# First attention of a fused linear-attention and MLP kernel: two token halves from the output products on, and small products of zeros in front

## The chip, the core and the metric

The kernel runs on one NeuronCore of a Trainium2 chip. A core has a matrix engine (TensorE, "PE" in the profile; its weight loads are "PEld"), a vector engine (VectorE, "DVE"), a scalar engine (ScalarE, "ACT"), a general engine (GpSimd, "POOL") and SyncE ("SP"), which issues transfers. Each engine works through a list of instructions of its own, and they wait for each other by semaphores. Transfers between the large memory (HBM) and the on-chip memory (SBUF) run on 16 DMA engines. Products land in a third memory, PSUM[...].

The metric is the device time of one execution in microseconds (us), the median of several. The profile is of one execution; its span is slightly shorter than the timed value.

## What is computed

```python
# q, k, v: (8, 8, 576, 64)   batch, heads, sequence, head dimension
kv  = np.einsum('bhsd,bhse->bhde', k, v)
out = np.einsum('bhsd,bhde->bhse', q, kv)
rms = np.sqrt(np.mean(out * out, axis=-1, keepdims=True) + 1e-06)
x   = out / rms * g_norm          # then (B,H,S,D) -> (B*S, H*D) = (4608, 512)
h   = x @ w_in                    # (512, 2048)
y   = np.maximum(0.01 * h, h) @ w_out
```

It is attention without a softmax, each head's output is divided by its root mean square, and a two-layer MLP follows. The weights `w_in` and `w_out` arrive as float64 numbers; the kernel rounds them to float32 itself, in two steps on ScalarE and four on VectorE for each block of weights. All products are float32; each shows in the trace as two records (two passes).

## The kernel before

The 4608 tokens are worked in nine blocks of 512. Block 0 is done plainly; blocks 1 to 8 use a Strassen scheme that the change leaves alone. Before block 0's MLP can start, the first 512 rows of x must be there, and that is the work of `first_attention`, on which everything waits.

Its parts, in program order (names as in the trace; "..." marks cuts):

```python
def load_first():
    # 12 loads of 288 KB (q, k, v of four pairs of heads) on three queues:
    # ScalarE ("a"), SyncE ("s") and GpSimd ("g")
    ...

zeros = view(g_all[0], 0, NT)                 # NT = 512
nc.vector.memset(zeros[:, :64], 0.0)
nc.vector.memset(zeros[:, 64:], 0.0)
...
load_w(0, nc.sync, nc.scalar)                 # first block of w_in ("stage"), 4 transfers of 128 KB

def first_attention():
    idle = ps_m.tile([P, NT], F32, tag="hd", name="idle_ps")

    def keep_warm(n=NT):
        matmul(idle[:, :n], lhsT=zeros[:, :P], rhs=zeros[:, :n], start=True, stop=True)

    keep_warm()
    keep_warm()
    ...
    for p in range(NP):                       # NP = 4 pairs of heads
        ...                                   # TensorE transposes q ("q_ps", "rest_ps"),
        ...                                   # ScalarE and VectorE copy it into qT
    for m in range(2):
        if m:
            keep_warm()
        attention_kv(0, m, kv_ps)             # the kv products
    ...
    copy_kv(0, kv_ps)                         # VectorE, kv_ps -> kv
```

From there, the part that the change regroups. `e` is one of two halves of the head dimension (32 of 64), `l` one of two heads of a pair, `half` one of two halves of the 512 tokens (N2 = 256 each), and `pin` keeps an instruction in program order on its engine (every product is pinned too):

```python
    for e in range(2):
        o_products(0, 0, NT, e, o_ps[e])      # "o_ps": 16 products of 512 columns

    w0 = rounding(0)                          # a generator: one step of rounding at each next()
    for e in range(2):
        for l in range(2):
            pin(nc.scalar.activation(squares[e][l], o_ps[e][l], func=AF.Square))        # "sq"
            if e == 0:
                pin(nc.vector.tensor_scalar(x[:, 2 * l, :], o_ps[0][l], g_sb[:, 0:1], None,
                                            op0=ALU.mult))
    for half in range(2):
        add_up(half)                          # TensorE: sums over a head ("sum_ps<-sq,group")
    next(w0, None); next(w0, None)            # ScalarE: "add", "cut"
    for half in range(2):
        root(half)                            # ScalarE: square root ("flat")
    for l in range(2):
        pin(nc.scalar.activation(x[:, 2 * l + 1, :], o_ps[1][l], func=AF.Copy, scale=g_sb[:, 1:2]))
    for half in range(2):
        turn(half)                            # TensorE: "sum_ps<-ident,flat"
    next(w0, None); next(w0, None)            # VectorE: clamp, shift
    invert(0)                                 # VectorE: reciprocal ("roots")
    spread(0)                                 # TensorE: "inv_ps<-ident,roots", 16 products
    next(w0, None)                            # VectorE: sign
    invert(1)
    spread(1)
    for _ in w0:                              # VectorE: last step
        pass
    for half in range(2):
        for l in range(2):
            scale(half, l)                    # VectorE: x times the spread reciprocals
    for j in range(1, 5):
        round_w(j)                            # further blocks of weights
```

(The two `next` on one line stand on lines of their own in the kernel.) Then the MLP of block 0 begins, "h_ps" being the product with `w_in` and "o_acc" that with `w_out`; the first of them, n = 0, is itself made in two token halves:

```python
    for n in range(2 * NC * U + 1):
        ...
        parts = 2 if n == 0 else 1
        for part in range(parts):
            cols = slice(part * NT // parts, (part + 1) * NT // parts)
            for e in range(NE):               # NE = 4
                matmul(h_ps[:, cols], lhsT=w1_sb[h][c][:, u, e, :], rhs=x[:, e, cols], ...)
        ...                                   # ScalarE: leaky ReLU; then the product with w_out of n - 1
```

Of the kernel before, what the change touches and what calls it, by code (L numbers as in the profile page):

```python
# [9 lines left out]
F32 = mybir.dt.float32  # L10
U32 = mybir.dt.uint32
I64 = mybir.dt.int64
AF = mybir.ActivationFunctionType
AX = mybir.AxisListType
ALU = mybir.AluOpType
# [8 lines left out]
def kernel(  # L24
# [36 lines left out]
    nc = tc.nc  # L61
    B, H, S, D = q.shape
    DM, DF = w_in.shape
    P = 128
    NE = DM // P
    E = 32
# [3 lines left out]
    NT = 4 * P  # L70
    NB = B * S // NT
    N2 = NT // 2
# [15 lines left out]
    ps_m = ctx.enter_context(tc.tile_pool(name="ps_m", bufs=1, space=bass.MemoryType.PSUM))  # L88

    pin = tc.keep_in_program_order  # L90
# [14 lines left out]
    def view(t, lo, *shape):  # L105
        n = 1
        for d in shape:
            n *= d
        t = t[:, lo:lo + n]
        names = "abcd"[:len(shape)]  # L110
        return t.rearrange(f"p ({' '.join(names)}) -> p {' '.join(names)}",
                           **dict(zip(names, shape))) if len(shape) > 1 else t
# [4 lines left out]
    def matmul(*args, **kw):  # L117
        pin(nc.tensor.matmul(*args, **kw))  # L118
# [4 lines left out]
    def half_of(p, i):  # L123


        return i ^ (p & 1)
# [58 lines left out]
    zeros = view(g_all[0], 0, NT)  # L185
# [26 lines left out]
    def load(t, src, eng):  # L212

        if len(src.shape) == len(t.shape):
            t, src = [t], [src]
        else:
            n = src.shape[1]
            t = [t[i * n:(i + 1) * n] for i in range(src.shape[0])]
        for i, (to, part) in enumerate(zip(t, src)):
            pin(eng[i * len(eng) // len(t)].dma_start(to, part))  # L220

    def load_f64(src, eng):
        a, n = src.shape[-2:]
        n //= 2
        raw = next(raw_homes).bitcast(U32).rearrange("p (n two) -> p n two", two=2)
        load(raw.rearrange("p (a n) two -> p a (n two)", a=a), src, eng)
        return raw
# [42 lines left out]
    def load_w(j, *eng):  # L270
        eng = eng or (nc.sync,)
        dst, src = w_jobs[j]
        if w_in.dtype == I64:
            w_raws[j] = load_f64(src.bitcast(U32), eng)
        else:
            load(dst, src, eng)
# [5 lines left out]
    def round_w(j):  # L282
        for _ in rounding(j):
# [8 lines left out]
    nc.vector.memset(group, 0.0)  # L292
    nc.vector.tensor_reduce(group[:, :NP], ident.rearrange("p (a i) -> p a i", i=E), axis=AX.X,
                            op=ALU.add)
    load_w(0, nc.sync, nc.scalar)
    g_sb = consts.tile([P, 2], F32, name="g_sb")
    for p in range(NP):
        pin(nc.gpsimd.dma_start(g_sb[p * E:(p + 1) * E], g_norm.rearrange("(e i) -> i e", i=E)))
# [35 lines left out]
    def o_products(b, lo, hi, e, o_ps):  # L334
        for p in range(NP):
            for l in range(2):
                r = slice(64 * l, 64 * l + 64)
                matmul(o_ps[half_of(p, l)][E * p:E * p + E, :],
                       lhsT=kvs[b % 2][r, p, E * e:E * e + E],
                       rhs=qTs[b][r, p, lo - b * S:hi - b * S], start=True, stop=True)  # L340
# [124 lines left out]
    def first_attention():  # L465


        idle = ps_m.tile([P, NT], F32, tag="hd", name="idle_ps")

        def keep_warm(n=NT):  # L470
            matmul(idle[:, :n], lhsT=zeros[:, :P], rhs=zeros[:, :n], start=True, stop=True)

        keep_warm()
        keep_warm()
        qT = qTs[0] = work.tile([P, NP, S], F32, tag="qT", name="qT")
        kv_ps = kv_tiles()


        rest = ps_m.tile([64, NP, P], F32, tag="oc", name="rest_ps")
        for j in range(1, 3):  # L480
            load_w(j)

        def move(p, l, to, of):

            c = 64 * half_of(p, l)
            eng = (nc.scalar.copy, nc.vector.tensor_copy)[l]
            eng(qT[c:c + 64, p, :].rearrange("p (t j) -> p j t", j=J)[:, to, :],
                of[:, :, 64 * l:64 * l + 64])

        for p in range(NP):  # L490
            q_in = q_ins.pop((0, p))
            banks = [ps_m.tile([64, 4, P], F32, tag=t, name="q_ps")
                     for t in (("ha", "hb"), ("hc", "oa"))[p % 2]]
            for j in range(J):
                to = banks[j // 4][:, j % 4, :] if j < 8 else rest[:, p, :]
                pin(nc.tensor.transpose(to, q_in[:, j, :], ident))
            for i in range(2):
                for l in range(2):
                    move(p, l, slice(4 * i, 4 * i + 4), banks[i])
        for p in range(NP):  # L500
            for l in range(2):
                move(p, l, slice(8, 9), rest[:, p:p + 1, :])
# [3 lines that stand above are left out]
            attention_kv(0, m, kv_ps)  # L506
        for j in range(3, 7):
            load_w(j)
        copy_kv(0, kv_ps)


        x = block(0)

        o_ps = [[ps_m.tile([P, NT], F32, tag=t, name="o_ps") for t in tags]
                for tags in (("hb", "hd"), ("oa", "oc"))]
        squares = [[spare(NT, "sq") for _ in range(2)] for _ in range(2)]
        roots = [work.tile([P, 2, 2, NP], F32, tag="rms", name="roots", bufs=2) for _ in range(2)]
        flat = [work.tile([64, N2], F32, tag="t2k", name="flat", bufs=3) for _ in range(2)]
        sum_ps = [ps_att.tile([P, NT], F32, tag="att", name="sum_ps") for _ in range(2)]
        inv_ps = [ps_m.tile([P, 2, N2], F32, tag=t, name="inv_ps") for t in ("ha", "hc")]  # L520
        for e in range(2):
            o_products(0, 0, NT, e, o_ps[e])

        def add_up(half):

            cols = slice(half * N2, half * N2 + N2)
            for e in range(2):
                for l in range(2):
                    matmul(sum_ps[half][E * l:E * l + E, :N2], lhsT=group,
                           rhs=squares[e][l][:, cols], start=(e == 0), stop=(e == 1))  # L530

        def root(half):

            pin(nc.scalar.activation(flat[half], sum_ps[half][:64, :N2], func=AF.Sqrt,
                                     scale=1.0 / D, bias=eps_sb[:64]))

        def turn(half):
            for t in range(2):
                matmul(turned(half)[:, t, :, :], lhsT=flat[half][:, t * P:t * P + P],
                       rhs=ident[:64, :64].rearrange("p (l i) -> p l i", l=2)[:, :, :NP],  # L540
                       start=True, stop=True)

        def turned(half):
            return sum_ps[half][:, N2:N2 + 4 * NP].rearrange("p (t l a) -> p t l a", t=2, l=2)

        def invert(half):
            pin(nc.vector.reciprocal(roots[half], turned(half)))

        def spread(half):

            for l in range(2):
                for t in range(2):
                    for p in range(NP):
                        matmul(inv_ps[half][E * p:E * p + E, l, t * P:t * P + P],
                               lhsT=roots[half][:, t, l, p:p + 1].to_broadcast([P, E]),
                               rhs=ident, start=True, stop=True)

        def scale(half, l):
            to = x[:, 2 * l:2 * l + 2, half * N2:half * N2 + N2]
            pin(nc.vector.tensor_tensor(  # L560
                to, to, inv_ps[half][:, l, :].unsqueeze(1).to_broadcast([P, 2, N2]), op=ALU.mult))

        w0 = rounding(0)
        for e in range(2):
            for l in range(2):
                pin(nc.scalar.activation(squares[e][l], o_ps[e][l], func=AF.Square))
                if e == 0:
                    pin(nc.vector.tensor_scalar(x[:, 2 * l, :], o_ps[0][l], g_sb[:, 0:1], None,
                                                op0=ALU.mult))
        for half in range(2):  # L570
            add_up(half)
        next(w0, None)
        next(w0, None)
        for half in range(2):
            root(half)
        for l in range(2):
            pin(nc.scalar.activation(x[:, 2 * l + 1, :], o_ps[1][l], func=AF.Copy,
                                     scale=g_sb[:, 1:2]))
        for half in range(2):
            turn(half)  # L580
        next(w0, None)
        next(w0, None)
        invert(0)
        spread(0)
        next(w0, None)
        invert(1)
        spread(1)
        for _ in w0:
            pass
        for half in range(2):  # L590
            for l in range(2):
                scale(half, l)
        for j in range(1, 5):
            round_w(j)

# [465 lines left out]
    x_sides, _, sums, _ = sides_x(1)  # L1061
# [34 lines left out]
    for i in range(1, NB):  # L1096
# [4 lines left out]
        for c in range(NC):  # L1101
# [76 lines left out]
            n = (i - 1) * NC + c  # L1178
# [36 lines left out]
```

## Time and profile before

| | |
|---|---|
| time, median of 3 | 919.92 us (919.35 to 920.18) |
| span of the profiled execution | 917.5 us |
| TensorE busy | 909.3 us, 99% of the span |
| VectorE busy | 631.9 us, 69% |
| GpSimd busy | 370.3 us, 40% |
| ScalarE busy | 328.4 us, 36% |
| HBM read, written | 172.39 MB, 26.48 MB |

A row of the profile's chain has a start, a duration (both us) and what ran, with the number of pieces merged into it. A row of the timeline has a start, a duration, the engine, the line of the kernel, the operation, and the tiles written and read. A row of the table by stretches has the stretch, its length, then for each engine the busy time and in brackets the number of instructions (TensorE, weight loads, VectorE, ScalarE, GpSimd), then TensorE's granted clock as a share of full speed, the busy share of the DMA engines and GB/s. L118 is the helper through which every product goes, so products are told apart by their tiles.

### The profile page before, as it was taken

What the parts mean: (1) busy time and instruction counts of PE and PEld (TensorE: products, weight loads), DVE (VectorE), ACT (ScalarE), POOL (GpSimd) and SP (SyncE); (2) the same over time, 40 slices, a digit from 0 to 9 for tenths busy, and PEclk for the clock granted to TensorE, in tenths of its full rate; (3) what the DMA queues carried; (4) which work ended last, traced back from release to release, by engine and by line L of the source; (5) the groups of instructions that cost most, each with busy time, mean ns of one, the idle gap of its engine ahead of it and who ended that gap; (6) DMA issues with size and microseconds to landing.
All of it is one profiled execution on the core that took longest, in us unless ns stands there. A gap on an engine that the chain in (4) does not pass through costs nothing.

```text
span 917.5 us, 18027 instructions
## 1 busy us (share of the span) xinstructions
PE 909.3 (99%) x6990; PEld 777.1 (85%) x6990; DVE 631.9 (69%) x1160; ACT 328.4 (36%) x649; POOL 370.3 (40%) x438
## 2 busy tenths in 40 slices
PE   8999999999999999999999999999999999999998
PEld 5444448888998999899998999999999999999997
DVE  4876995587457876587767875687569755755565
ACT  5454533242144233533343323342343333223330
POOL 2000355966633562236322632264226522542222
PEclk9999999999999999999999999999999999999999
DMA  9999926885598679856986699658755676667632
GB/s 262 227 260 245 249 93 193 277 277 167 168 334 281 182 224 284 276 173 200 299 236 227 178 285 269 229 174 251 242 180 172 193 218 201 184 187 221 200 109 92
DMA packets 90229, 200.06 MB, mean 218 GB/s; under 512 B 9888, under 2 KB 42272, under 8 KB 90144
## 3 DMA queue, kind: packets, MB, share of 16 engines
q1 hardware_dynamic: 79680, 187.04, 69.2%
q10 hardware_dynamic: 10016, 10.69, 3.4%
q8 instruction: 56, 0.92, 0.4%
q0 software_dynamic: 448, 1.18, 0.3%
q14 instruction: 29, 0.24, 0.1%
HBM read 172.39 MB, written 26.48 MB: 217 GB/s over the span
## 4 chain that ended last, share of the span: by engine, by line
PE 95%; DMA 3%; DVE 1%; POOL 1%; issue 0%; ACT 0%; DVEq 0%; POOLq 0%; ACTq 0%
PE o_a L118 18%; PE o_c L118 18%; PE h_ha L118 11%; PE h_hb L118 10%; PE h_hc L118 8%; PE h_hd L118 8%; PE o_acc L118 6%; PE h_ps L118 6%; PE o_ps L118 2%; PE kv_ps L118 2%; PE h_a L118 1%; PE h_c L118 1%; DMA pairs<-in_v_dram 1%; PE h_b L118 1%; PE h_d L118 1%; DMA w<-pairs 1%
## 5 line engine op out<-in xcount | busy, mean ns | idle before, releaser
L598 POOL TENSOR_TENSOR gs<-g 128x512 f32<-128x512 f32 x64 | 81.9, 1280 | 250.8 <-ACT g L794 250.8
L794 ACT ACTIVATE g<-g 128x512 f32<-128x512 f32 x124 | 78.2, 631 | 132.3 <-DVE g L598 132.3
L913 ACT COPY w_all<-h_ha 128x512 f32<-128x512 f32 x84 | 48.8, 581 | 171.7 <-PE h_ha L118 166.1
L118 PE MATMUL o_a<-pairs,gs 128*128 128x256 f32 x384 | 91.3, 381 | 0.0
L118 PE MATMUL o_c<-pairs,gs 128*128 128x256 f32 x376 | 89.6, 381 | 0.0
L598 DVE TENSOR_TENSOR o<-h_hb,o 128x128 f32<-128x128 f32 x104 | 29.9, 287 | 84.0 <-ACT pairs L913 82.9
L598 DVE TENSOR_TENSOR o<-o_c,o 128x512 f32<-128x512 f32 (+1 forms) x91 | 61.3, 673 | 27.2 <-PE o_c L118 26.9
L118 PEld LDWEIGHTS o_a<-pairs,gs 128*128 128x128 f32 x384 | 69.8, 190 | 10.9 <-POOL pairs L598 3.1
L118 PEld LDWEIGHTS o_c<-pairs,gs 128*128 128x128 f32 x376 | 68.3, 190 | 7.9
L598 DVE TENSOR_TENSOR o<-o_a,o 128x512 f32<-128x512 f32 x75 | 51.3, 684 | 29.0 <-PE o_a L118 28.8
L118 PE MATMUL h_ha<-stage,w_all 128*128 128x128 f32 x448 | 59.6, 276 | 0.0
L598 POOL TENSOR_TENSOR pairs<-w_all 128x512 f32<-128x512 f32 x8 | 11.1, 1384 | 120.2 <-DMA stage<-in_moe_w_in_dram 91.8
L118 PEld LDWEIGHTS h_ha<-stage,w_all 128*128 128x128 f32 x448 | 56.6, 192 | 3.0 <-issue 0.9
L118 PE MATMUL h_ps<-xT,w_all 128*128 128x512 f32 (+1 forms) x136 | 57.7, 569 | 0.7 <-DVE xT L560 0.7
L118 PE MATMUL o_acc<-w,g 128*128 128x512 f32 x128 | 57.8, 595 | 0.0
L598 POOL TENSOR_TENSOR pairs<-g 128x128 f32<-128x128 f32 x52 | 24.2, 465 | 82.7 <-PE h_hb L118 52.9
L598 DVE TENSOR_TENSOR g<-g,pairs 128x512 f32<-128x512 f32 x84 | 55.7, 689 | 1.9
L118 PEld LDWEIGHTS h_ps<-xT,w_all 128*128 128x128 f32 x136 | 25.5, 190 | 29.5 <-issue 26.3
L118 PEld LDWEIGHTS o_acc<-w,g 128*128 128x128 f32 x128 | 24.0, 190 | 29.8 <-issue 29.4
L598 DVE TENSOR_TENSOR w_all<-h_hc,w_all 128x512 f32<-128x512 f32 x56 | 38.3, 685 | 14.1 <-PE h_hc L118 14.0
L598 DVE TENSOR_TENSOR o<-h_hd,o 128x128 f32<-128x128 f32 x78 | 22.2, 284 | 36.1 <-ACT pairs L913 35.7
L118 PE MATMUL h_hb<-stage,w_all 128*128 128x128 f32 x336 | 46.7, 275 | 0.0
(225 smaller groups left out, 2263.4 us busy)
## 6 DMA issues: line engine op xcount, KB each, us to landing
w_all<-w SPq DMA_DIRECT2D x196, 448.0 KB, 4.3
pairs<-w SPq DMA_DIRECT2D x56, 512.0 KB, 4.3
out_dram<-o ACTq DMA_DIRECT2D x35, 256.0 KB, 5.3
v_in<-in_v_dram SPq DMA_DIRECT2D x29, 288.0 KB, 5.8
k_in<-in_k_dram SPq DMA_DIRECT2D x28, 288.0 KB, 5.9
q_in<-in_q_dram SPq DMA_DIRECT2D x56, 144.0 KB, 6.3
q_in<-in_q_dram SPq DMA_DIRECT2D x56, 140.0 KB, 6.1
w<-stage SPq DMA_DIRECT2D x12, 512.0 KB, 4.5
```

The source lines that it names most:

```text
L118: pin(nc.tensor.matmul(*args, **kw))
L598: ins = eng.tensor_tensor(out_, a, b_, op=ALU.subtract if minus else ALU.add)
L794: nc.scalar.activation(t, t if src is None else src, func=AF.Prelu, alpha=SLOPE)
L913: nc.scalar.copy(q[:, at], bank)
```

## The change

From the output products on, the first attention is worked in two halves of 256 tokens: each half has its output products for both `e`, its squares, sums, roots, reciprocals and scaling, and the order of these steps on the engines is rewritten so that work of one half stands beside that of the other. The purpose is to have the first 256 rows of x ready early and to scale the other 256 while the first product of the MLP is under way, since that product is made in two token halves itself. To this end the PSUM tiles are cut by half instead of by `e`; the multiplication by g of half 0 is on VectorE, that of half 1 on ScalarE.

In front, two products of zeros of 512 columns, which keep TensorE active until the first q has landed, become forty of 4 columns with 32 stationary columns. The first block of `w_in` is loaded by SyncE's queue alone, no longer by SyncE's and ScalarE's. The whole diff:

```diff
--- before.py
+++ after.py
@@ -292,7 +292,7 @@
     nc.vector.memset(group, 0.0)
     nc.vector.tensor_reduce(group[:, :NP], ident.rearrange("p (a i) -> p a i", i=E), axis=AX.X,
                             op=ALU.add)
-    load_w(0, nc.sync, nc.scalar)
+    load_w(0)
     g_sb = consts.tile([P, 2], F32, name="g_sb")
     for p in range(NP):
         pin(nc.gpsimd.dma_start(g_sb[p * E:(p + 1) * E], g_norm.rearrange("(e i) -> i e", i=E)))
@@ -467,11 +467,11 @@
 
         idle = ps_m.tile([P, NT], F32, tag="hd", name="idle_ps")
 
-        def keep_warm(n=NT):
-            matmul(idle[:, :n], lhsT=zeros[:, :P], rhs=zeros[:, :n], start=True, stop=True)
-
-        keep_warm()
-        keep_warm()
+        def keep_warm(n=NT, m=P):
+            matmul(idle[:m, :n], lhsT=zeros[:, :m], rhs=zeros[:, :n], start=True, stop=True)
+
+        for _ in range(40):
+            keep_warm(4, 32)
         qT = qTs[0] = work.tile([P, NP, S], F32, tag="qT", name="qT")
         kv_ps = kv_tiles()
 
@@ -511,23 +511,25 @@
 
         x = block(0)
 
-        o_ps = [[ps_m.tile([P, NT], F32, tag=t, name="o_ps") for t in tags]
+        o_ps = [[ps_m.tile([P, 2, N2], F32, tag=t, name="o_ps") for t in tags]
                 for tags in (("hb", "hd"), ("oa", "oc"))]
         squares = [[spare(NT, "sq") for _ in range(2)] for _ in range(2)]
         roots = [work.tile([P, 2, 2, NP], F32, tag="rms", name="roots", bufs=2) for _ in range(2)]
         flat = [work.tile([64, N2], F32, tag="t2k", name="flat", bufs=3) for _ in range(2)]
         sum_ps = [ps_att.tile([P, NT], F32, tag="att", name="sum_ps") for _ in range(2)]
-        inv_ps = [ps_m.tile([P, 2, N2], F32, tag=t, name="inv_ps") for t in ("ha", "hc")]
-        for e in range(2):
-            o_products(0, 0, NT, e, o_ps[e])
+        inv_ps = [[ps_m.tile([P, N2], F32, tag=t, name="inv_ps") for t in tags]
+                  for tags in (("ha", "hc"), ("hb", "hd"))]
+        for half in range(2):
+            for e in range(2):
+                o_products(0, half * N2, half * N2 + N2, e, [o[:, e, :] for o in o_ps[half]])
 
         def add_up(half):
 
-            cols = slice(half * N2, half * N2 + N2)
             for e in range(2):
                 for l in range(2):
                     matmul(sum_ps[half][E * l:E * l + E, :N2], lhsT=group,
-                           rhs=squares[e][l][:, cols], start=(e == 0), stop=(e == 1))
+                           rhs=squares[half][l][:, e * N2:e * N2 + N2], start=(e == 0),
+                           stop=(e == 1))
 
         def root(half):
 
@@ -551,45 +553,61 @@
             for l in range(2):
                 for t in range(2):
                     for p in range(NP):
-                        matmul(inv_ps[half][E * p:E * p + E, l, t * P:t * P + P],
+                        matmul(inv_ps[half][l][E * p:E * p + E, t * P:t * P + P],
                                lhsT=roots[half][:, t, l, p:p + 1].to_broadcast([P, E]),
                                rhs=ident, start=True, stop=True)
 
+        def of_x(half, l):
+            return x[:, 2 * l:2 * l + 2, half * N2:half * N2 + N2]
+
+        def by_g(half, l):
+            to, of = of_x(half, l), o_ps[half][l]
+            if half == 0:
+                pin(nc.vector.tensor_tensor(to, of, g_sb.unsqueeze(2).to_broadcast([P, 2, N2]),
+                                            op=ALU.mult))
+                return
+            for e in range(2):
+                pin(nc.scalar.activation(to[:, e, :], of[:, e, :], func=AF.Copy,
+                                         scale=g_sb[:, e:e + 1]))
+
         def scale(half, l):
-            to = x[:, 2 * l:2 * l + 2, half * N2:half * N2 + N2]
+            to = of_x(half, l)
             pin(nc.vector.tensor_tensor(
-                to, to, inv_ps[half][:, l, :].unsqueeze(1).to_broadcast([P, 2, N2]), op=ALU.mult))
+                to, to, inv_ps[half][l].unsqueeze(1).to_broadcast([P, 2, N2]), op=ALU.mult))
+
+        def square(half, l):
+            pin(nc.scalar.activation(squares[half][l],
+                                     o_ps[half][l].rearrange("p e n -> p (e n)"),
+                                     func=AF.Square))
 
         w0 = rounding(0)
-        for e in range(2):
-            for l in range(2):
-                pin(nc.scalar.activation(squares[e][l], o_ps[e][l], func=AF.Square))
-                if e == 0:
-                    pin(nc.vector.tensor_scalar(x[:, 2 * l, :], o_ps[0][l], g_sb[:, 0:1], None,
-                                                op0=ALU.mult))
-        for half in range(2):
-            add_up(half)
+        for half, l in ((0, 0), (0, 1), (1, 0)):
+            square(half, l)
+        add_up(0)
+        for l in range(2):
+            by_g(0, l)
+        root(0)
+        square(1, 1)
+        add_up(1)
+        turn(0)
         next(w0, None)
         next(w0, None)
-        for half in range(2):
-            root(half)
+        root(1)
         for l in range(2):
-            pin(nc.scalar.activation(x[:, 2 * l + 1, :], o_ps[1][l], func=AF.Copy,
-                                     scale=g_sb[:, 1:2]))
-        for half in range(2):
-            turn(half)
+            by_g(1, l)
+        invert(0)
+        spread(0)
+        turn(1)
         next(w0, None)
         next(w0, None)
-        invert(0)
-        spread(0)
-        next(w0, None)
+        scale(0, 0)
+        scale(0, 1)
+        for _ in w0:
+            pass
         invert(1)
         spread(1)
-        for _ in w0:
-            pass
-        for half in range(2):
-            for l in range(2):
-                scale(half, l)
+        for l in range(2):
+            scale(1, l)
         for j in range(1, 5):
             round_w(j)
 
```

## The prediction

> **What bounds the kernel now.** I read the page's busy shares first, then the busy time of three stretches (start, first matmuls of the first block, the rest).
>
> ```profile
> PE 909.3 (99%) x6990; PEld 777.1 (85%) x6990; DVE 631.9 (69%) x1160; ACT 328.4 (36%) x649; POOL 370.3 (40%) x438
> ...
> 0.00:24.00 24.00, 19.58 (x307) 12.68 (x307) 11.99 (x30) 14.25 (x28) 5.16 (x14) 1.00 0.91 262
> 24.00:34.40 10.40, 10.40 (x33) 6.08 (x34) 9.97 (x19) 6.42 (x12) 0.00 (x0) 1.00 1.09 224
> 34.40:917.50 883.10, 879.27 (x6653) 758.34 (x6651) 609.94 (x1112) 307.72 (x611) 365.17 (x424) 1.00 0.73 217
> ```
>
> The first number after the comma is TensorE's busy time. After 24.00 us it is busy 889.67 of 893.50 us at a granted clock of 1.00, and the change touches nothing there. So the whole question is by how much the first-block products start earlier or later, and whether they then run without a hole: any shift of that stream should arrive at the end. I therefore read the chain that ended last, over the first stretch:
>
> ```profile
> 3.70 9.23 DMA pairs<-in_v_dram
> ...
> 13.07 1.45 PE kv_ps L118 x72
> 14.52 0.28 DVE kv L322
> ...
> 14.94 2.04 PE o_ps L118 x32
> ...
> 18.33 2.46 PE sum_ps L118 x19
> ...
> 21.42 1.05 PE inv_ps L118 x32
> ...
> 22.56 1.30 DVE xT L560 x2
> 23.86 0.14 issue
> 23.99 7.13 PE h_ps L118 x24
> ```
>
> Up to 12.94 us the chain is the last load of v. Then it is a relay between engines: products, squares, sums, roots, turning, reciprocals, spreading, scaling, and at 23.99 the first product with w1. The relay takes 23.99 - 14.94 = 9.05 us, and that is what the halves are meant to shorten. The timeline of VectorE shows what lies just behind it:
>
> ```profile
> 23.77 1.28 DVE L560 TENSOR_TENSOR xT<-xT,inv_ps 128x512 f32<-128x512 f32 x2
> 24.96 0.42 DVE L247 TENSOR_SCALAR cut<-cut 128x512 f32<-128x512 f32 x1
> 25.41 0.43 DVE L251 TENSOR_SCALAR w_all<-cut 128x512 uint32<-128x512 uint32 x1
> 25.88 0.69 DVE L253 SCALAR_TENSOR_TENSOR w_all<-cut,w_all 128x512 uint32<-128x512 uint32 x1
> 26.60 0.69 DVE L256 CUSTOM_DVE_ANT_0 w_all<-w_all,add 128x1024 uint16<-128x1024 uint16 x1
> ```
>
> These four rows after the scaling round the second block of w1, and end at 27.29. The product that needs it (n = 1) starts at 27.52 (16 half products of 0.216 after 23.99). So only 0.23 us separate VectorE from becoming the bound: were the first product to start earlier, the second would wait for this rounding.
>
> **What the Trainium skill says.** Its page "TensorE: Matmul & The Clock Gate", section "Step-by-step: what each phase is for", says that matmuls stay in program order and only weight loads are pulled ahead. The trace agrees: the order of the products is the program's throughout. The change's new order is therefore binding. The same page, "What's actually happening", puts the warm-up at about 3.4 us of activity, by time and not by count. Here the first product starts at 1.53 and the transposes fall from 213 to 109 ns apart at about 6.65 us, 5.1 us later. "TensorEngine Tiling (Array Packing)", section "Instruction Overhead", gives about 60 cycles to a small matmul, however few its columns; no run so far shows one of 4 columns. "DMA: Bandwidth & Descriptors", section "Issuing engines are not separate DMA queues", says that a second issuing engine saves only issue time. Here the two issues on ScalarE took 338 and 317 ns.
>
> **The change, part by part.** *The front.* Two products of zeros of 512 columns go: four records, 0.854 us apart, from 1.53 to about 5.0. Forty of 4 columns by 32 come: eighty records. They need only the first memset, which ends at 1.00, so they can start near 1.05. At 60 cycles, with the cold rate of the removed ones (512 columns in 854 ns, two cycles per column, so 0.83 ns per cycle, an estimate from these and the page), eighty take about 4.0 us and end near 5.1, where the first q lands (5.01). The transposes would start at 5.1 as now, perhaps warm a little sooner. I choose to credit this with nothing. The transposes end at 9.96 and the copies of q at 13.63, while the products that read them can't start before the v load (12.94), 1.4 us of kv products and a copy, at 14.94. *The load of w0 on one queue* takes two issues from ScalarE, which now hold its first copy of q back to 6.48; that too ends ahead of 14.94, and w0 is rounded late in both kernels. I keep 14.94 for the first output product, give or take 0.2.
>
> *The halves.* I follow the new program order on each engine with durations of the kernel before. Eight records of 512 columns run side by side per 0.43 us, so eight of 256 take 0.215.
>
> 1. The first half needs 4 x 0.215 us of products, just as much as the first e now. So the first square starts where it does now, 16.2. Three squares at a pitch of 0.49: ends at 16.8, 17.3, 17.8.
> 2. The sums of half 0 wait for the second square (17.3) and not, as now, for the fourth (18.3). From release to root took 1.1 us (18.31 to 19.42), so the root starts at 18.4 and ends at 18.9. This is the gain: one us.
> 3. It is lost at once. On ScalarE the fourth square comes *after* this root: 18.8 to 19.4. On TensorE the sums of half 1, which need that square, stand *ahead* of the turning of half 0. They release at 19.4; the last is issued at 19.4 + 3 x 0.215 = 20.05; the turning follows after the change of array shape (0.31 now, 19.87 to 20.18) at about 20.4. Now it is 20.18. Its reciprocal starts 0.71 later, 21.1 (now 20.89), and ends at 21.35.
> 4. VectorE has done its two multiplications by g at 18.3 and idles till 21.1, because the reciprocal stands ahead of the first steps of rounding w0. In the kernel before those steps (0.43 + 0.43) fill this very gap. Now they come after it, 21.3 to 22.2.
> 5. The spreading of half 0: reciprocal's end + 0.15 (VectorE to TensorE, as 14.79 to 14.94), 32 of the 64 records that took 1.68 us, 0.27 for the last: ready at 22.65. Two scalings, pitch 0.6: to 23.9.
> 6. The rest of rounding w0, 0.6 + 0.7: to 25.2. Then the reciprocal of half 1, to 25.45. Only then the spreading of half 1: 25.6 to 26.4 for its issue.
> 7. The first product with w1 stands behind that spreading, so it starts at about 26.6 (now 23.99), although its own inputs are ready at 25.2. Its first half (8 x 0.216 = 1.73) hides the two scalings of half 1 (26.75 to 28.0), as intended, and it ends at about 30.05.
> 8. Rounding the second block of w1 starts after these scalings, at 27.95, and takes 2.33 as now: 30.3. With 0.15 to TensorE, product n = 1 starts at 30.4; now 27.52.
>
> Sum: +2.9 us at product n = 1, of which 2.6 are already there at the first product. As a check by VectorE's work alone: from the first multiplication by g to the end of that rounding it now has 10.43 us with 1.6 idle, so 8.85 of work, which the change keeps. The new order has idle stretches of 2.8 (step 4), 0.5 (before the first scaling) and 1.3 (before the third), 4.6 in all, and 4.6 - 1.6 = 3.0. From there on the deadlines are looser (the rounding after it is ready at 29.54 and needed at 30.96), and VectorE and TensorE shift together. Nothing later on gives it back: TensorE has 3.8 us of idle in 883. 919.92 + 2.9 = **922.8 us**.
>
> **The rivals.** *The halves work as meant*: the second pair of scalings (2 x 0.6 = 1.2 us) goes beside the first product, and the chain of half 0 is a us shorter. That would start n = 0 at 22 to 23 and give 918 to 919. For it speaks step 2; against it the order in steps 3 and 6, and that the rounding of w1's second block would take part of it. *Something else than order holds the sums*: in the trace only one record of the sums runs at 16.91, and all others start at 18.33, though the second and third squares were done at 17.3 and 17.8. If this strange hold is what cost a us, and the new grouping avoids it in both halves, half 1 is 0.4 earlier than I have it: 922.3. *A colder clock*: the products of zeros are small, and if they don't count as activity, the transposes run at half speed for up to 3.4 us more. Thirty-six at 109 ns more each are 3.9 at most, of which the wait for v hides about 1.3 (from 13.63 to 14.94). I think 0 to 0.5 of it likely. Also, in step 6 TensorE idles some 2.5 us (after the turning of half 1, at 23.1, up to 25.6); if the clock fell there, n = 0 would run at half speed, another 1.7 to 3.5: 924.5 to 926. Against it: the longest idle of TensorE in the trace after its start is 1.02 us, so no run shows such a gap, but it is shorter than the window of the page. *Transfers*: with ScalarE's queue empty sooner, v may land up to 0.2 earlier.
>
> **Range and chances.** The middle of my working is 922.8. Latencies that I carried over add about +-0.7, the repeats of the kernel before spread over 0.8. The hold and the transfers pull down to 921, the clock up to 924.6. Range 921.0 to 924.6. Two per cent would be 18.4 us, twice the relay itself: faster 0.01, within 0.98, slower 0.01.
>
> **What would show it.** In the profile after: the first square still near 16.2; root of half 0 near 18.4; turning of half 0 near 20.4; VectorE idle from 18.3 to 21; reciprocal of half 1 only near 25.2, behind the rounding; first product with w1 near 26.6 instead of 23.99, with its second half not waiting; product n = 1 released by VectorE's rounding near 30.4; then the same busy TensorE at clock 1.00. I am wrong if the first product starts before 24.5, if the copies of q or the kv products end later than now (the front matters after all), if a clock below 1.00 shows in the first 35 us, or if idle time later in the span takes the shift back.

## The result, and the profile after

The changed kernel takes **925.28 us** (median of 4, 921.78 to 926.36), the kernel before 919.85 us (median of 4, 919.35 to 920.18): a ratio of 1.0054, 95% interval 1.0034 to 1.0074. It is slower by half a per cent, and the time lies 0.7 us above the predicted range. The profiled execution has a span of 924.0 us against 917.5. The extra 6.5 us fall into four stages:

| stage | before | after | difference |
|---|---|---|---|
| start to the first output product ("o_ps") | 14.94 | 17.20 | +2.26 |
| relay: from there to the first product with w1 ("h_ps") | 9.05 | 11.92 | +2.87 |
| from there to the first product with w2 ("o_acc") | 6.97 | 9.09 | +2.12 |
| the rest | 886.5 | 885.8 | -0.8 |

First the busy time by stretches of the changed kernel, the same three columns to be read as before (length, then TensorE's busy time; third from the end the granted clock):

```profile
0.00:24.00 24.00, 19.52 (x358) 15.55 (x362) 8.89 (x24) 12.00 (x25) 5.17 (x14) 1.00 0.86 250
24.00:34.40 10.40, 8.47 (x83) 6.77 (x72) 8.70 (x16) 5.29 (x10) 0.00 (x0) 0.67 1.09 206
34.40:45.00 10.60, 10.60 (x27) 4.89 (x26) 9.06 (x18) 5.72 (x10) 0.00 (x0) 1.00 1.09 213
```

In the second stretch TensorE is no longer full, and its clock is 0.67 on average: the trace shows half speed from 26.58 to 33.41 us. The timeline of TensorE shows the order of the relay:

```profile
15.33 1.40 PE L118 MATMUL kv_ps<-pairs 64*64 64x64 f32 x72 [1.55 <-DMA pairs<-in_v_dram]
17.20 2.06 PE L118 MATMUL o_ps<-qT,kv 64*32 64x256 f32 x64 [0.47 <-DVE kv L322]
19.19 1.54 PE L118 MATMUL sum_ps<-sq,group 128*32 128x256 f32 x10
21.70 1.05 PE L118 MATMUL sum_ps<-sq,group 128*32 128x256 f32 x6 [0.98 <-ACT sq L579]
22.68 0.61 PE L118 MATMUL sum_ps<-ident,flat 64*128 64x8 f32 x4
23.71 1.08 PE L118 MATMUL inv_ps<-ident,roots 128*32 128x128 f32 x32 [0.42 <-DVE roots L549]
24.72 0.61 PE L118 MATMUL sum_ps<-ident,flat 64*128 64x8 f32 x4
27.26 1.93 PE L118 MATMUL inv_ps<-ident,roots 128*32 128x128 f32 x32 [1.93 <-DVE roots L549]
29.12 9.25 PE L118 MATMUL h_ps<-xT,w_all 128*128 128x256 f32 x24
```

A bracket is idle time of the engine before the row, and what ended it. The second kv products wait for v until 15.33 (before: 13.07). The sums of half 1 wait 0.98 us for the fourth square, and the turning of half 0 comes only behind them. The second spreading waits 1.93 us for VectorE. It takes 1.93 us for 32 records where the first took 1.08, and the 24 records of "h_ps" take 9.25 us instead of 7.13: both are the low clock. VectorE's timeline says what it did meanwhile:

```profile
19.10 1.29 DVE L566 TENSOR_TENSOR xT<-o_ps,g_sb 128x512 f32<-128x512 f32 x2 [1.85 <-ACT sq L579]
23.40 0.26 DVE L549 RECIPROCAL roots<-sum_ps 128x16 f32<-128x16 f32 x1 [3.01 <-PE sum_ps L118]
...
26.34 0.69 DVE L256 CUSTOM_DVE_ANT_0 w_all<-w_all,add 128x1024 uint16<-128x1024 uint16 x1
26.95 0.25 DVE L549 RECIPROCAL roots<-sum_ps 128x16 f32<-128x16 f32 x1
28.48 0.69 DVE L575 TENSOR_TENSOR xT<-xT,inv_ps 128x512 f32<-128x512 f32 x1 [1.27 <-PE inv_ps L118]
```

It stands still for 3.01 us ahead of the first reciprocal, and makes the second only after the last step of rounding w0.

### The profile page after: what moved, and what is told of

Same layout as the page of the kernel before. It is cut to its first block, busy times and chain, and to the rows that moved or that the text cites. A ratio compares the mean times of both kernels' runs of the same rounds, so it can differ in the third digit from the quotient of the medians.

```text
span 924.0 us, 18244 instructions
## 1 busy us (share of the span) xinstructions
PE 914.2 (99%) x7098; PEld 783.8 (85%) x7098; DVE 633.3 (69%) x1160; ACT 329.3 (36%) x651; POOL 371.2 (40%) x438
## 4 chain that ended last, share of the span: by engine, by line
PE 95%; DMA 2%; DVE 1%; ACT 1%; issue 0%; SPq 0%; ACTq 0%; DVEq 0%
PE o_a L118 19%; PE o_c L118 18%; PE h_ha L118 11%; PE h_hb L118 10%; PE h_hc L118 8%; PE h_hd L118 8%; PE h_ps L118 6%; PE o_acc L118 6%; PE o_ps L118 2%; PE kv_ps L118 2%; PE h_a L118 2%; PE h_b L118 1%; DMA stage<-in_moe_w_in_dram 1%; PE h_c L118 1%; PE h_d L118 1%; DVE g L616 0%
## 5 line engine op out<-in xcount | busy, mean ns | idle before, releaser
L118 PE MATMUL h_ps<-xT,w_all 128*128 128x512 f32 (+1 forms) x136 | 59.8, 588 | 0.0
```

## The experiments

Three causes are to be kept apart: the front (late v), the order of the relay, and the fall of the clock. The table has what the profile of each run shows, in us, beside its time. The fetch column is the start of the first 16 KB transfer on the instruction queue, from the trace's list of packets; the relay and the next column are stages two and three of the table above. The experiments ran on three chips, e1 to e4, e5 to e8 and e9 to e12 on one each, always beside the kernel before. There its own executions spread more than in the result (beside e1 to e4 from 918.4 to 927.9 us, 63 of them, median 922.3). Three executions of 1581 to 1916 us (two of e3, one of the kernel before beside e5 to e8) are left out. Ratios are to the kernel before beside the run, and the stages are read from the profiles. The changed kernel's repeat, e6, is only 0.17% slower by its ratio, and the interval reaches 1, although its three stages together are 5.8 us longer than in the first profile of the kernel before; the end of this part comes back to that.

| run | fetch | last k or v landed | first o_ps | relay | h_ps to o_acc | time (n) | ratio, 95% interval |
|---|---|---|---|---|---|---|---|
| before (result) | 15.4 | 12.94 | 14.94 | 9.05 | 6.97 | 919.85 (4) | |
| changed (result) | 8.5 | 15.20 | 17.20 | 11.92 | 9.09 | 925.28 (4) | 1.0054 [1.0034, 1.0074] |
| e1 halves only | 15.5 | 12.65 | 14.65 | 14.23 | 7.73 | 925.30 (20) | 1.0033 [1.0018, 1.0048] |
| e2 front only | 8.5 | 15.52 | 17.52 | 8.65 | 6.96 | 922.45 (12) | 1.0006 [0.9978, 1.0035] |
| e3 forty only | 10.3 | 13.81 | 15.86 | 8.64 | 6.96 | 920.43 (18) | 0.9985 [0.9962, 1.0007] |
| e4 one queue only | 15.3 | 13.53 | 15.53 | 8.65 | 6.96 | 920.94 (20) | 0.9990 [0.9972, 1.0008] |
| e5 before again | 15.4 | 12.81 | 14.81 | 8.96 | 6.96 | 922.24 (1) | |
| e6 changed again | 9.6 | 15.03 | 17.03 | 11.48 | 8.21 | 925.06 (20) | 1.0017 [0.9998, 1.0037] |
| e7 TensorE filled | 8.7 | 13.79 | 15.81 | 11.06 | 7.00 | 923.25 (12) | 1.0000 [0.9970, 1.0031] |
| e8 order mended | 8.6 | 13.95 | 15.74 | 8.46 | 7.07 | 922.15 (20) | 0.9993 [0.9971, 1.0015] |
| e9 sixteen | 15.2 | 12.85 | 15.30 | 12.31 | 6.96 | 922.01 (1) | |
| e10 reciprocal moved | 8.9 | 13.81 | 16.37 | 10.50 | 7.69 | 923.92 (12) | 1.0007 [0.9981, 1.0032] |
| e11 forty behind | 15.1 | 12.91 | 19.71 | 10.21 | 6.96 | 924.32 (1) | |
| e12 mended, 32 columns | 8.6 | 13.72 | 15.72 | 8.45 | 7.06 | 922.25 (12) | 1.0000 [0.9972, 1.0027] |

### The parts alone (e1 to e4)

**e1**: the relay of the changed kernel with the front of the kernel before.

```diff
-        for _ in range(40):
-            keep_warm(4, 32)
+        keep_warm()
+        keep_warm()
...
-    load_w(0)
+    load_w(0, nc.sync, nc.scalar)
```

> The halves alone; the front (two products of zeros of 512 columns, first block of weights on two queues) as before. Theory (order of the relay): the first output product stays near 14.9 us and the last v near 12.9, the first product with w1 starts 2.8 us later than before after its output products (11.8 instead of 9.05), and TensorE idles nearly 2 us before the spreading of half 1. If the clock does not fall in that idle: about 922.2; if it falls: about 924. Rival (the front is the cause of most): within 0.5 us of before.

**e2**: the reverse, the front of the changed kernel with the relay of the kernel before. **e3** has of the front only the forty products, **e4** only the single queue.

> The front alone (forty small products of zeros, first block of weights on one queue); the relay as before. Theory (the front delays the last v, in whole or in part through an instruction fetch of 16 KB that occupies one DMA engine): last v near 15.2 instead of 12.9, first product with w1 near 26.2, about 922.0. Rival (the late v of the changed kernel was chance, or comes from the halves): 919.9 within 0.4.

> The forty small products alone, weights on two queues as before. Theory (instruction fetch): an instruction fetch of 16 KB near 8.5 us as in the changed kernel, last v near 15, about 922. Rival (the single queue delays v): last v near 12.9, 919.9. In both the transposes run at the low clock up to about 9.4.

> The first block of weights on one queue alone. Theory (instruction fetch): no fetch before 15 us, last v near 12.9, 919.9. Rival (the single queue delays v): last v near 15.2, about 922.

The slowdown comes with the halves: e1 is 0.33% slower than the kernel before, and the three kernels without halves are not distinguishable from it. For e2 the interval runs from -2.0 to +3.2 us. So the expectation for e2 (2 us slower) isn't confirmed by the time, although the late v is there in the profile (15.52). The forty alone bring the fetch forward (10.3) and v lands at 13.81, 1.2 us later than in e1 (12.65), which has the old front; but the single queue alone, without an early fetch, has 13.53, where 12.9 was expected, so it may have a share of its own.

e1 brought a surprise. Its relay is even longer than the changed kernel's, by a hold in the midst of the output products. Here is TensorE's timeline of e1:

```profile
14.65 1.24 PE L118 MATMUL o_ps<-qT,kv 64*32 64x256 f32 x33 [0.47 <-DVE kv L322]
18.32 1.09 PE L118 MATMUL o_ps<-qT,kv 64*32 64x256 f32 x31 [2.43 <-issue]
```

After 33 of 64 records it stands still for 2.43 us, and "issue" says that nothing which the profile shows ended this. The kernel before has such a hold too, the strange one of the prediction's second rival:

```profile
16.91 0.40 PE L118 MATMUL sum_ps<-sq,group 128*32 128x256 f32 x1
18.33 1.92 PE L118 MATMUL sum_ps<-sq,group 128*32 128x256 f32 x15 [1.02 <-issue]
```

The work is different, but if TensorE's records (weight loads, products, and the waits on semaphores between them) are counted from the start, both holds come ahead of the 449th, and both end at 18.3 us, 2.9 us after a 16 KB transfer on the instruction queue began (both at 15.45). That suggests that TensorE waits there for its own instructions. e5, e9 and e11 test it.

### A wait for instructions (e5, e9, e11)

**e5** is the kernel before, unchanged.

> The kernel before once more, for a profile from the chip of these runs. If the hold of the sums is a wait for instructions that arrive as one block, TensorE stands still again ahead of the same instruction or, where the block comes in time, not at all; the relay from the first output product to the first product with w1 is 9.05 us or 8.65 us. Rival (the hold is a rule of waits on semaphores): the same hold of 1.0 us whatever the time of the instruction block.

It holds again ahead of record 449, for 0.91 us, until 18.10. (Its span is 2.9 us longer than that of the first profile, for another reason: 2.54 us of waiting for a later load of v, as its timeline of TensorE says.)

```profile
90.61 1.27 PE L118 MATMUL kv_ps<-v_in,k_in 64*64 64x64 f32 x70 [2.54 <-DMA v_in<-in_v_dram]
```

**e9** shifts the count by 60 records without changing the work behind:

```diff
         ...
         keep_warm()
-        keep_warm()
+        for _ in range(16):
+            keep_warm(4, 32)
```

> The kernel before with the second large product of zeros replaced by sixteen of 4 columns by 32: as long in time, but 60 TensorE records more ahead of everything else. Theory (TensorE waits for a block of instructions that begins at its 449th record): the hold moves from the sums to the output products, ahead of the third to fifth record of them, and ends near 18.2 us as in the kernels before; v near 12.9, because this is too few extra records for an early fetch. Rival (the hold belongs to the sums and their semaphores): the output products run through and the hold is again after the first record of the sums.

TensorE's timeline of e9:

```profile
15.30 1.02 PE L118 MATMUL o_ps<-qT,kv 64*32 64x512 f32 x3 [0.51 <-DVE kv L322]
18.23 2.56 PE L118 MATMUL o_ps<-qT,kv 64*32 64x512 f32 x29 [1.91 <-issue]
```

The hold moved to where it was expected: after three records of the output products, again ahead of record 449, 1.91 us, and it ends at 18.23. (The relay of e9, 12.31 us, also holds 3.4 us of half speed, from 19.42 on.) **e11** puts the forty behind the transposes:

```diff
             ...
             if m:
                 keep_warm()
+            else:
+                for _ in range(40):
+                    keep_warm(4, 32)
```

> The kernel before with both large products of zeros in front and the forty small ones behind the transposes, ahead of the first kv products. Theory (forty small products in front bring the fetch of instructions to 8.5 us and with it delay v): with them behind the transposes the fetch comes at 10.5 or later, so v lands near 13.0. If the fetch even comes only near 15.4, TensorE stands still within the second kv products until about 18.2 and the first output product starts near 19.5; if it comes near 10.5 to 12, nothing stands still. Rival (forty small products delay v wherever they are): v near 14 to 15.5.

TensorE's timeline of e11:

```profile
16.08 1.11 PE L118 MATMUL kv_ps<-pairs 64*64 64x64 f32 x26
17.68 1.55 PE L118 MATMUL kv_ps<-pairs 64*64 64x64 f32 x46 [0.48 <-issue]
```

Now the hold is in the second kv products, ahead of record 450, and ends at 17.68, 2.5 us after the fetch began (15.13). In five profiles of four kernels the hold thus follows the count and not the operation. The rival, a rule of waits on semaphores, has fallen: the kernels e2, e3 and e4 have the same sums and the same waits and no hold. In e4 the fetch is as late as in the kernel before (15.3), but v is later too, so that record 449 comes only at 18.03 us, 2.8 us after the fetch began, which is when the holds end elsewhere. That the transfer holds TensorE's instructions is inferred from this count and timing; its content is not in the trace.

e11 speaks on v as well. It has the same eighty records of products, only later, and no early fetch; v lands at 12.59 and the last k at 12.91. In the six profiles without a fetch before 15 us the last load lands between 12.65 and 13.53, in the eight with one between 13.72 and 15.52. A count of the queues over the first 12 us of the changed kernel shows the transfer, whose line is absent in the kernel before and in e11:

```profile
q0 software_dynamic: 363, 1.17, 25.1%
q8 instruction: 1, 0.02, 0.6%
```

It is one packet of 16 KB that occupies one DMA engine for 1.1 us, at 8.49. In the list of packets of the changed kernel the last packets of k and v then come singly, 0.1 to 0.4 us apart, from 11.7 to 13.1 us, as from one engine that lags; in the kernel before the last one starts at 11.67. e3, with two queues and the early fetch, has such single packets too, until 12.71; e4, with one queue and no early fetch, has none, and its packets end together at 12.10. So the early fetch delays v by such stragglers, and the single queue seems to shift the loads as a whole. How large each share is stays open: with both, the last load lands at 15.0 to 15.5 in three profiles (changed, e2, e6) and at 13.7 to 14.0 in four (e7, e8, e10, e12).

What the front gives and takes is now visible: with the halves and the old front (e1) TensorE is held for 2.43 us in the output products; with the forty in front the fetch comes early and this hold is gone, but v is later: by about as much in the changed kernel and e6 (15.20 and 15.03 against 12.65), by half of it in e7 and e10 (13.79 and 13.81).

### The clock and the order (e6, e7, e8, e10, e12)

**e6** is the changed kernel once more. **e7** keeps TensorE at work ahead of the second spreading:

```diff
         turn(1)
+        for _ in range(4):
+            matmul(inv_ps[1][0], lhsT=zeros[:, :P], rhs=zeros[:, :N2], start=True, stop=True)
```

> The changed kernel once more. Theory (front delays v through an early instruction fetch, order of the relay costs 2.9, the clock falls in most executions): fetch of 16 KB near 8.5 us, last v between 14 and 15.5, relay 11.9, clock below 1.00 from about 27 us, time 924 to 926. Rival (the late v was chance): last v near 13.

> The changed kernel with four products of zeros of 256 columns put into TensorE's idle time ahead of the spreading of half 1. Theory (that idle time lets the clock fall, and the fall costs about 2): clock 1.00 throughout, relay 11.9 as before it, first product at 3.5 us per 16 half products, 2 us less than the changed kernel beside it. Rival (the clock falls for another reason): clock still below 1.00, same time.

TensorE's timeline of e7:

```profile
23.87 1.99 PE L118 MATMUL inv_ps<-g 128*128 128x256 f32 x8
25.86 1.08 PE L118 MATMUL inv_ps<-ident,roots 128*32 128x128 f32 x32
26.87 4.58 PE L118 MATMUL h_ps<-xT,w_all 128*128 128x256 f32 x18
```

The second spreading is back at 1.08 us, the relay is 11.06, and "h_ps" to "o_acc" takes 7.00. So of the changed kernel's excess the low clock is 0.86 in the relay (11.92 - 11.06) and 2.09 behind it (9.09 - 7.00), together 2.95 us in that profile with its 6.83 us of half speed; in e6, with 3.41 us of it, 0.42 and 1.21. In 19 of 20 executions of e6 the mean clock over the span was below 1.000, in 4 of 12 of e7. (In the kernel before beside them it was so in 23 of 46; the mean does not say where the clock fell, and in e3 and e12 it fell at 92 to 93 us.) The median of e7 is 1.8 us below e6, and 2 were expected.

**e8** keeps the halves and the front, and mends the order. The rounding makes "cut" ahead of "add", and:

```diff
         for l in range(2):
             by_g(0, l)
+        next(w0, None)
         root(0)
         square(1, 1)
+        turn(0)
         add_up(1)
-        turn(0)
         next(w0, None)
         next(w0, None)
+        next(w0, None)
+        invert(0)
+        spread(0)
         root(1)
         for l in range(2):
             by_g(1, l)
-        invert(0)
-        spread(0)
         turn(1)
-        next(w0, None)
-        next(w0, None)
-        scale(0, 0)
-        scale(0, 1)
         for _ in w0:
             pass
+        scale(0, 0)
         invert(1)
         spread(1)
+        scale(0, 1)
```

> The changed kernel with the same halves but another order: cutting the high words ahead of the first root; turning of half 0 ahead of the sums of half 1; the clamp and shift of w0 ahead of the reciprocal of half 0; all of the rounding of w0 ahead of the first scaling; one scaling ahead of the reciprocal of half 1. Theory (order, not halving, costs the 2.9): relay 8.8 instead of 11.9, no fall of the clock, 4 to 5 us less than the changed kernel, level with the kernel before plus the late v. Rival (halving costs by itself, by more and smaller instructions): relay above 10.5.

TensorE's timeline of e8:

```profile
22.17 0.61 PE L118 MATMUL sum_ps<-ident,flat 64*128 64x8 f32 x4
23.19 1.08 PE L118 MATMUL inv_ps<-ident,roots 128*32 128x128 f32 x32 [0.42 <-DVE roots L549]
24.20 6.37 PE L118 MATMUL h_ps<-xT,w_all 128*128 128x256 f32 x22
```

The wait ahead of the second spreading falls from 1.93 to 0.42 and the relay to 8.46, 3.46 less than in the changed kernel (0.86 of that was the low clock) and 0.2 below the relay of the kernels without halves and hold (8.65). So it is the order that costs, not the halving. By its median the time is 2.9 us below e6, where 4 to 5 were expected. **e10** makes only one of the moves, reciprocal and spreading of half 1 ahead of the second scaling and the rest of the rounding:

```diff
         scale(0, 0)
+        invert(1)
+        spread(1)
         scale(0, 1)
         for _ in w0:
             pass
-        invert(1)
-        spread(1)
```

> The changed kernel with one move: reciprocal and spreading of half 1 come after the first scaling of half 0, ahead of the second scaling and of the rest of rounding w0. Theory (that order costs most of the relay's 2.9): TensorE's idle time of 1.9 us ahead of the second spreading shrinks below 0.5, relay 10.2 instead of 11.9, clock mostly 1.00, about 2 to 3 us less than the changed kernel. Rival (VectorE's total work bounds the first product, whatever the order): relay within 0.5 of 11.9.

TensorE's timeline of e10:

```profile
24.91 1.94 PE L118 MATMUL inv_ps<-ident,roots 128*32 128x128 f32 x32 [0.42 <-DVE roots L549]
```

The wait is 0.42 again and the relay 10.50, of which 0.86 is a second spreading at low clock (1.94 us instead of 1.08). The clock fell at 24.93 although no idle of TensorE from 21.85 on exceeds 0.42 us. It isn't that one idle stretch alone, then. What else counts stays open: TensorE was busy 2.59 of the 3.43 us ahead of this fall, but the changed kernel had as little, 2.42 of 3.40 us from 19.80 on, and its clock did not fall at the end of that stretch. Of e10's 12 executions only 3 have a mean clock of 1.000, where it was expected to be so in most.

**e12** is e8 with forty products of 32 columns in place of 4.

> The kernel with the mended order, and the forty products of zeros with 32 columns in place of 4, which should take no longer while the clock is low (each record 53 ns apart; 32 columns at 1.67 ns are 53). Theory (products of 4 columns do not count as activity for the clock, so it rises only 3.4 us or more after the transposes begin; with more columns streamed they count): clock 1.00 from about 7 us instead of 9 to 11, transposes ended near 10.2 instead of 11.3 to 12.4, relay 8.5, time level with the kernel with the mended order, as all of this lies ahead of v. Rival (the late rise is chance, or is due to the 32 stationary columns): clock 1.00 only from 9 us or later.

The first rows of TensorE's timeline, the changed kernel and then e12:

```profile
1.06 4.43 PE L118 MATMUL idle_ps<-g 128*32 128x4 f32 x80 [1.06 <-DVE g L186]
5.42 1.92 PE L496 MATMUL q_ps<-ident,q_in 128*64 128x128 f32 x8
```

```profile
1.06 4.02 PE L118 MATMUL idle_ps<-g 128*32 128x32 f32 x80 [1.06 <-DVE g L186]
5.01 1.06 PE L496 MATMUL q_ps<-ident,q_in 128*64 128x128 f32 x8
```

With 32 columns the first transposes already run at full speed (1.06 us for eight instead of 1.92), and the clock is recorded as full from 4.30; with 4 columns it is so only from 9.52. e11 shows the same from the other side, in the busy time by stretches:

```profile
10.70:14.10 3.40, 3.40 (x144) 3.31 (x141) 2.08 (x6) 1.44 (x5) 0.00 (x0) 1.00 0.56 155
14.10:24.30 10.20, 9.24 (x115) 4.10 (x112) 1.90 (x4) 1.83 (x4) 0.00 (x0) 0.50 0.83 215
```

TensorE is busy 3.40 of 3.40 us, mostly with products of 4 columns, and at the end of it the clock falls for three times 3.4 us. Neither mended kernel can be told from the kernel before by its time (0.9993 and 1.0000, each within 0.3% by its interval): what they win in the relay the profiles show lost with the late v (0.2 to 0.6 against about 0.8).

A second reason why the times differ less than the stages is the wait that e5 showed at 90.61. There TensorE comes to kv products of a later block, which need another load of v. The first profile of the kernel before has no wait at this place:

```profile
87.97 1.28 PE L118 MATMUL kv_ps<-v_in,k_in 64*64 64x64 f32 x72
```

Its load had landed at 86.70 already; in e5 TensorE was there at 87.74 and the load landed at 90.47. Waits of 1.38, 2.05, 2.46, 0.41, 2.41 and 4.47 us stand at the same place in e2, e3, e4, e8, e10 and e12. The changed kernel and e1, e6, e7, e9 and e11 come there later, at 90.9 to 95.2, find the load landed and do not wait. So part of what a quicker relay wins is lost again at this wait, and part of what a slower one loses would have been waited for there anyhow. No run separates how much. The four executions of the kernel before in the result (919.35 to 920.18), one of them profiled without this wait, lie low among its later ones, and the 5.4 us between the medians there are more than the 2.7 us between those of e6 and the kernel before beside it (922.4).

## Why the prediction was wrong

- **The front** is the step that failed (with the clock, below): "I choose to credit this with nothing", "I keep 14.94 for the first output product". It came at 17.20, +2.26, and how late v lands varies between profiles of this front (13.7 to 15.5), so the size is in part chance. The cadence was right (54 ns a record, the last ended at 5.5 for 5.1). That the copies and transposes don't matter held only because v was later still: the last copy of q ended at 14.94 instead of 13.63. What the working left out is the transfer of 16 KB on the instruction queue, which runs beside the loads: 160 records (products and weight loads) in 4.4 us bring it into the middle of the k and v loads. And "perhaps warm a little sooner" was the wrong way round: products of 4 columns did not raise the clock, and the transposes ended 1.4 us later than before, as the third rival had it.
- **The relay's order**, steps 1 to 4: right to within 0.1. Counted from the first output product, the first square comes at 1.27 (worked out: 1.26), the first root at 3.50 (3.46), the turning of half 0 at 5.48 (5.46), the first reciprocal at 6.20 (6.16).
- **Steps 5 to 7**: the mechanism right, the size smaller. The second reciprocal comes at 9.75, not 10.26, as the first scaling starts at 7.22 after the first output product and not 7.71. At full clock (e7) the first product with w1 is at 11.06 instead of 11.66: the order costs 2.0, not 2.6, against the kernel before with its hold, and 2.4 against a relay without hold (8.65). The check by VectorE's work did not bear the 2.9 out: the idle time that it put at 1.6 us is 2.0 in the trace (8.42 busy of 10.43), which makes the difference 2.6.
- **Step 8**, that product n = 1 would wait for the rounding of w1: not seen. In the changed kernel that rounding is done at 32.27 and n = 1 starts at 34.78, as n = 0 is still running at low clock. In e7 the rounding is done at 30.18 and n = 1 starts at 30.43, right behind n = 0.
- **The rival of the clock** was named, with its place and size (1.7 to 3.5, "924.5 to 926"), and set aside because the idle time expected, 2.5 us, was shorter than the window that the prediction cites. The longest idle time was 1.93 us, shorter still, and the clock fell all the same: the measurement goes against that argument. It came true with 2.95 us: 2.09 in n = 0, as named, and 0.86 in the second spreading.
- **The rival of the hold** was open; by e9 and e11 it is a wait for instructions. The halves would have made it worse (2.43 for 1.02), and the forty take it away.
- **"Nothing later on gives it back"** held for the two profiles of the result (rest -0.8) but not beyond: of the stages of e6, 6.0 us longer than those of e5, 2.7 us are left between the medians of the two kernels. That this is close to the predicted 2.9 is chance.

As a sum for the profiled execution: late v 2.26, order 2.01 (11.06 - 9.05), clock 2.95, rest -0.8, together 6.4 of 6.5 us. Of the -0.8, 0.49 is a later wait for k and v at 168.6 us that the kernel before has in its profile and the changed one has not; the other 0.3 was not traced.

Open: what decides when the fetch starts. With forty products in front it starts at 8.5 to 10.3, in all others at 15.1 to 15.5. In none of the fourteen profiles does it start before TensorE's record 193, which is 256 records ahead of the hold; the forty bring this record forward (6.6 to 8.5 us instead of 10.7 to 11.9). But the fetch follows it after 0.1 to 2.0 us with them and after 3.2 to 4.7 without, and why is not shown.

## What to carry to other kernels

In a chain between engines, an instruction's place in its engine's order is a dependency: read, for each engine, what stands ahead of the next link of the chain, and put waiting work behind it. Count the instructions of an engine as well as their time: many small products in a row can run into a wait for the next block of instructions, which shows as idle time ended by "issue" at the same count in kernels of different work, and a fetch in the midst of large loads can delay them. Look also for the next wait behind the stage that you shorten: it can take the gain back. To keep TensorE's clock up, give it products that stream columns, and look at the granted clock after any change that thins out its work.

## What the runs showed of the hardware that was not expected

- In four of these kernels TensorE stood still ahead of its 449th or 450th record for 0.5 to 2.4 us, until 2.5 to 3.0 us after a transfer of 16 KB on the instruction queue had begun.
- Eighty product records of 4 columns, 4.4 us without a gap, left the clock low until 9.5 us (8.6 to 11.3 in the five other profiles with them that recorded it); eighty of 32 columns at nearly the same pace (4.0 us) had it high at 4.3 in one profile, and four of 512 columns, in 3.8 us, at 4.7 to 7.3 in five.
- The clock fell in stretches of 3.41 us and multiples (3.41, 6.83, 10.24), in one case with no idle of TensorE over 0.42 us in the 3 us ahead.
